# The last block's output projection as seven half-size products per pair of units, with a longer pause between two halves of the scan's outputs

## Chip, cores, metric

The kernel runs on one core of a Trainium2 chip. The metric is the time of one execution on the device in microseconds (us), the median of three runs. The core's engines each take their instructions in order: PE multiplies matrices (PEld loads its weights beside it), DVE, ACT and POOL work on tiles, SP starts DMA transfers. They run beside one another and wait for each other by semaphores.

## What is computed

A decaying scan in chunks over `x` (attention without softmax), whose result goes through a gated two-layer product:

```python
# scan, per batch and head, by chunks: M = (C B^T) * decay, causal
y[:, :, sl] = M @ xc + (C @ state) * decay_to_i
state = decay_full * state + sum(B x decay_from_j)
# y, regrouped to 3072 tokens of 256, is the x of
g = x @ w_gate                       # 256 -> 1536
val = x @ w_val                      # 256 -> 1536
out = (g * sigmoid(g) * val) @ w_out # 1536 -> 256
```

All of it is fp32. A product of two fp32 matrices is made of three products of their rounded high parts and the remainders: w_high·x_high, w_high·x_low, w_low·x_high. So each operand is split first: ACT rounds it to the high part, and DVE or POOL subtracts that from the whole for the low part.

## The kernel before

The tokens go in 6 blocks, k = 0 to 5, of 512 columns. For each, the scan writes four tiles y (`S`, `L`, `st` and `y` in the trace), and the gated product follows. The hidden layer is cut into 12 slices of 128, two slices making a pair j = 0 to 5. From block 3 on, gate and value of a pair are computed by seven products of half size each (units (k, j, m), m = 0 gate, m = 1 value; `stage1a`, `stage1b`, `stage2`, `stage3`): PE writes tile `pq` and tile `r`, ACT copies (`sp<-pq`), POOL adds (`sp<-sp`, the function `both`), DVE subtracts (`sp<-r,sp`, `carry`) and finishes (`pq<-pq,sp`; `hp<-pq,hp`). The result is the pair's hidden tile `hp`, 128 x 4 x 256 columns, in fp32.

`pair_high` (ACT, 128x1024) and two `pair_low` (POOL, 128x512) split it into `ph` and `pl`. Then `project` multiplies by the output weights `wo`, high and low: per slice and per half m of the outputs three matmuls of 512 columns, summed over the 12 slices in the PSUM banks `po5_0` and `po5_1`. In the last block the last four slices (HB = 4) of `po5_1` go in two halves of 256 columns. That makes 60 matmuls of 512 columns and 24 of 256. ACT and DVE copy the banks to `ob` (`drain`, `drain_part`), and SP stores these (`store`).

No loop sets the order on the engines: every step is added to a `Plan` with an engine (or `EITHER(pool, dve)`, two engines with a cost on each), a cost, a due time, what it needs, and the slots it takes and gives back. The plan simulates the engines and writes each one's order, which `Ordered` then keeps; all operations pass through its line, L206 in the trace (L205 after the change). Steps of the pretended engine `Page` are pauses: one stands between the two halves of the outputs y of a block (`values_and_sums`, `carried_and_values`), and in it PE takes other matmuls, those of the block before.

Of the kernel before, what the change touches and what calls it, by code (L numbers as in the profile page):

```python
# [9 lines left out]
F32 = mybir.dt.float32  # L10
# [17 lines left out]
NP = H // 2  # L28
NF = DFF // P
SG = 23  # L30
HB = 4
RAW = 8
PR = 3
FAST = 3
# [182 lines left out]
def scan_moe_kernel(ctx: ExitStack, tc, aj, an, bc, xb, wgv, wo, cst, own, first_e, e_table, out):  # L217
# [654 lines left out]
    def pair_low(k, j, i):  # L872
# [47 lines left out]

    def sums_of(k):

        if k < NB - 1:
            return [(m, (0, T), (f,)) for f in range(NF) for m in range(2)]
        early, late = NF - HB, tuple(range(NF - HB, NF))
        runs = [(0, (0, T)), (1, (0, T // 2)), (1, (T // 2, T))]
        return [(m, (0, T), (f,)) for f in range(early) for m in range(2)] + [(m, t, late) for m, t in runs]

    def project(k, m, t, fs):
        if (k, m) not in tot:  # L930
            tot[k, m] = ps_mm.tile([P, T], F32, tag="mm", name=f"po{k}_{m}")
        for f in fs:
            r, e = divmod(f, 2)
            o = tot[k, m][:, t[0] : t[1]]
            if k < FAST:
                hh, hl = (hid[k, f][n][:, t[0] : t[1]] for n in ("hh", "hl"))
            else:
                a = slice(t[0] // TH, t[1] // TH)
                hh, hl = (
                    hid[k, r, n].rearrange("p (a b) t -> p a b t", b=2)[:, a, 1 - e] for n in "hl"  # L940
                )
# [10 lines left out]
    def drain(k, m, t, e):  # L952
        obs[k, m, t] = moe.tile([P, T], F32, tag="ob", name=f"ob{k}_{m}_{t[0]}", bufs=2)
        copy(e, obs[k, m, t][:, : t[1] - t[0]], tot[k, m][:, t[0] : t[1]])

    def drain_part(k, m, t, i, e):
        if (k, m, t) not in obs:
            obs[k, m, t] = moe.tile([P, T], F32, tag="ob", name=f"ob{k}_{m}_{t[0]}", bufs=2)
        n = (t[1] - t[0]) // 2
        copy(e, obs[k, m, t][:, n * i : n * i + n], tot[k, m][:, t[0] + n * i : t[0] + n * i + n])  # L960

    def store(k, m, t):
        sp.dma_start(out[k, P * m : P * m + P, t[0] : t[1]], obs[k, m, t][:, : t[1] - t[0]])
# [31 lines left out]
    def do(f, *a):  # L995
# [83 lines left out]
    def fast_x(k, z, y, done):  # L1079
# [7 lines left out]
        for n, (i, ms) in enumerate(((2, ()), (1, ("M1",)), (0, ("M3",)), (3, ("M4",)))):  # L1087
# [42 lines left out]
    for k in range(NB):  # L1130
# [132 lines left out]
    for k in range(NB):  # L1263
        prev = None
        for n, (m, t, fs) in enumerate(sums_of(k)):
            b = ("po", k, m)
# [7 lines left out]
            if fs[-1] == NF - 1:  # L1274
                o = ("ob", k, m, t)
                c = 0.6 * (t[1] - t[0]) / T
                if t[0]:
                    parts = [("ob", k, m, t, i) for i in range(2)]
                    add("-", 0.0, lambda: None, r, [prev], takes=[("ob", o)], gives=("held", o))
                    for i, e in enumerate(("Act", "DVE")):  # L1280
                        add([(e, c / 2)], None, do(drain_part, k, m, t, i), r + 0.5, [("held", o)], uses=[b, o], gives=parts[i])
                    add("SP", 0.48, do(store, k, m, t), r + 2, parts, uses=[o], gives=("stored", k, m, t), lag=0.9)
                    continue
                add([("Act", c)] + ([("DVE", c)] if k < FAST - 1 or k == NB - 1 else []), None, do(drain, k, m, t), r + 0.5, [prev], takes=[("ob", o)], uses=[b, o], gives=o)
# [147 lines left out]
```

## Time and profile before

| what | value |
| --- | --- |
| median of three runs | 339.67 us (338.07, 341.18, 339.67) |
| the profiled execution: its time, its span | 338.35 us, 336.6 us |
| mean granted clock of PE in it | 1.000 of full speed |
| PE busy | 329.8 us |
| DVE, ACT, POOL busy | 230.7, 175.8, 177.5 us |

The span runs from the first to the last instruction; the profiled execution's own time is 1.75 us above it. Busy times are of the whole span; a stage may have another limit.

### The profile page before, as it was taken

The page shows a single profiled execution, that of the slowest core. Times are in us where ns is not written, and L with a number is a line of the kernel's source. Part 1 is how long each engine was busy: PE and PEld are TensorE (multiplying, and loading weights), DVE is VectorE, ACT ScalarE, POOL GpSimd, SP SyncE. Part 2 cuts the span into 40 slices and gives each one's busy share as a digit, 9 for nine tenths or more (in the row PEclk, how much of TensorE's full clock was granted, in tenths as well). Part 3 has the DMA queues.
Part 4 walks back from the last instruction along what each step waited for, and adds up shares of the span by engine and source line. Part 5 has one row for each costly group of instructions (what it writes and reads, how often), then busy time and mean ns, then how long its engine had stood idle before and what let it go on. Part 6 is the DMA issues. An engine that isn't in the chain of part 4 may idle for free.

```text
span 336.6 us, 8407 instructions
## 1 busy us (share of the span) xinstructions
PE 329.8 (98%) x3506; PEld 276.0 (82%) x3506; DVE 230.7 (69%) x410; ACT 175.8 (52%) x324; POOL 177.5 (53%) x164
## 2 busy tenths in 40 slices
PE   7999999999999999999999999989999999999995
PEld 5645758888888888878888999868999878999985
DVE  7999999879699981475298577735777834376600
ACT  5797967654245534544382666312666342566411
POOL 2487743510223009897979998350368341368450
PEclk9999999999999999999999999999999999999999
DMA  7899986990001841000292000008400000100001
GB/s 247 288 384 238 293 182 209 248 220 19 1 2 44 194 145 63 1 2 2 52 233 82 14 2 2 2 4 232 148 1 0 5 2 2 62 2 0 2 0 62
DMA packets 10100, 31.05 MB, mean 92 GB/s; under 512 B 1455, under 2 KB 2223, under 8 KB 9423
## 3 DMA queue, kind: packets, MB, share of 16 engines
q1 hardware_dynamic: 7192, 24.21, 24.0%
q0 software_dynamic: 1440, 2.88, 4.8%
q10 hardware_dynamic: 1431, 3.43, 3.5%
q8 instruction: 27, 0.44, 0.5%
q14 instruction: 10, 0.08, 0.1%
HBM read 24.29 MB, written 3.35 MB: 82 GB/s over the span
## 4 chain that ended last, share of the span: by engine, by line
PE 98%; DMA 1%; issue 0%; DVE 0%; ACTq 0%; ACT 0%
PE gv L206 31%; PE po L206 30%; PE pq L206 23%; PE y L206 6%; PE r L206 4%; PE S L206 2%; PE a L206 1%; DMA rows<-in_aj 1%; PE st L206 0%; ACTq L1426 0%; PE rest L206 0%; DVE rows L206 0%; PE e L206 0%; DVE ob L206 0%; ACT ob L206 0%
## 5 line engine op out<-in xcount | busy, mean ns | idle before, releaser
L206 POOL TENSOR_TENSOR pl<-hp,ph 128x512 fp32r<-128x512 f32 x36 | 46.6, 1306 | 28.7 <-PE po L206 24.2
L206 POOL TENSOR_TENSOR sp<-sp 128x256 f32<-128x256 f32 x36 | 27.7, 772 | 33.1 <-ACT sp L206 30.9
L206 DVE TENSOR_TENSOR pq<-pq,sp 128x512 f32<-128x512 f32 x36 | 25.0, 697 | 21.5 <-PE pq L206 21.5
L206 ACT COPY sp<-pq 128x512 f32<-128x512 f32 x36 | 20.9, 588 | 22.9 <-PE pq L206 22.7
L206 DVE TENSOR_TENSOR_SCAN L<-L,dj 128x520 f32<-128x520 f32 x20 | 27.1, 1399 | 4.9 <-DMA L<-clipped 4.9
L206 ACT ACTIVATE sg<-gv 128x512 f32<-128x512 f32 x36 | 21.4, 596 | 15.8 <-PE gv L206 15.4
L206 DVE TENSOR_TENSOR sg<-gv,sg 128x512 f32<-128x512 f32 x28 | 19.1, 683 | 11.1 <-PE gv L206 8.3
L206 ACT ACTIVATE hp<-pq 128x512 f32<-128x512 f32 x36 | 20.1, 601 | 10.5 <-DVE pq L206 8.9
L206 ACT COPY ob<-po 128x512 f32<-128x512 f32 (+2 forms) x13 | 7.0, 545 | 35.1 <-PE po L206 34.6
L206 DVE TENSOR_TENSOR hp<-pq,hp 128x512 f32<-128x512 f32 x36 | 23.5, 681 | 1.0 <-PE pq L206 0.6
L206 DVE TENSOR_TENSOR sp<-r,sp 128x256 f32<-128x256 f32 x36 | 15.0, 416 | 13.2 <-POOL sp L206 13.2
L206 ACT CAST ph<-hp 128x1024 fp32r<-128x1024 f32 x18 | 18.9, 1054 | 9.6 <-PE po L206 6.1
L206 ACT CAST hh<-sg 128x512 fp32r<-128x512 f32 x23 | 14.3, 622 | 14.0 <-PE po L206 9.7
L206 DVE TENSOR_TENSOR hh<-sg,hh 128x512 fp32r<-128x512 f32 x28 | 20.6, 760 | 0.8 <-ACT hh L206 0.7
L206 DVE TENSOR_TENSOR L<-S,L 128x512 f32<-128x512 f32 x24 | 15.1, 682 | 1.0 <-PE S L206 1.0
L206 PE MATMUL y<-L,xb 64*32 64x64 f32 x768 | 11.7, 232 | 1.0 <-issue 0.9
L206 PEld LDWEIGHTS y<-L,xb 64*32 64x32 f32 x768 | 9.2, 109 | 4.1 <-issue 1.7
L206 DVE TENSOR_TENSOR gv<-gv,sg 128x512 f32<-128x512 f32 x8 | 5.6, 700 | 10.1 <-PE gv L206 10.1
L206 ACT ACTIVATE Cz<-bc,cs 128x512 f32<-128x512 f32 x12 | 8.0, 716 | 4.6 <-DMA bc<-in_bc 4.6
L206 POOL TENSOR_TENSOR wt<-wg0h,wg0l 128x512 f32<-128x512 f32 x1 | 1.3, 1290 | 16.7 <-DVE xb L206 16.7
L206 POOL TENSOR_TENSOR wdl<-wd,wdh 128x512 fp32r<-128x512 f32 x6 | 8.2, 1366 | 3.6 <-ACT wdh L206 3.6
L206 DVE COPY ob<-po 128x128 f32<-128x128 f32 x1 | 0.3, 290 | 14.2 <-ACT ob L206 14.2
(673 smaller groups left out, 1118.3 us busy)
## 6 DMA issues: line engine op xcount, KB each, us to landing
L<-clipped SPq DMA_DIRECT2D x10, 520.0 KB, 10.3
xb<-in_xb SPq DMA_DIRECT2D x6, 768.0 KB, 12.3
bc<-in_bc SPq DMA_DIRECT2D x6, 512.0 KB, 5.9
out<-ob SPq DMA_DIRECT2D x11, 256.0 KB, 4.5
E<-clipped SPq DMA_DIRECT2D x5, 260.0 KB
wg0r<-in_wgv SPq DMA_DIRECT2D x1, 512.0 KB
wg1r<-in_wgv SPq DMA_DIRECT2D x1, 512.0 KB, 6.3
wg2r<-in_wgv SPq DMA_DIRECT2D x1, 512.0 KB
```

Of the source, the lines that this page charges most:

```text
L206: ins = getattr(self.engine, name)(*a, **k)
```

## The change

The last block's projection is computed as seven products of half size per pair, M1 to M7, in place of eight. One side of each product is a quarter of `wo` (M1, M2, M4) or a sum of quarters (M5, M7, M6, M3); the other is a quarter of `hp` or a mix of quarters. Three matmuls of 256 columns for each product and pair make 126 matmuls, summed over the pairs in four banks `pm0` to `pm3`.

- Sums of weights, per pair: `o_whole` adds high and low (128x512), four `o_sum` (128x128), `o_high` on ACT and `o_low` (128x512) split them into `os`. `o_whole` and `o_low` stand on POOL for pairs 0 and 4, and 0 and 5, and on DVE for the others; they use `spare` and `spare2`, tiles where the scan's `L` and `xb` were.
- Mixes of the hidden tile, per pair, all on DVE: "ends" (128x512), then "both" (128x256, into `hp`), then "last" (128x256).
- `pair_high` and `pair_low` give way to four `h_high` (ACT) and four `h_low` per pair, three of 128x512 and one of 128x256. The parts lie where weights lay that no step needs any more: `wg0h`, `wg0l` and so on, `ws`, `wdh`, `wdl`. The plan puts the low parts of 18 of the 24 on POOL, six on DVE (`wg1l`, `wdh1`, `wg7l`, `wdl4`, `wdh4`, `wg11l`).
- `join`: one copy on ACT and seven adds of 128x256 on DVE make the four quarters of the output from the banks; four stores of 128x256 follow.
- The pause between the two halves of y, from block 4 on, goes from 0.5 to REST = 2.8, and the slack of `values_and_sums` from 1.0 to 0.1. Ahead of the first half of y of block 4, PE then has four groups of three `po` matmuls (before: six), and six between the halves (before: four). For block 5 it is three groups and six (before: five and four).
- One idle matmul near the start is 256 columns wide (before: 512).

The core of the diff (the steps' costs in the plan, `new_spare` with the views of the tiles, and most of `join` are cut):

```diff
-HB = 4
+    PRODUCTS = ("M1", "M2"), ("M6", "M7"), ("M5", "M3"), ("M4",)
+    FACTORS = dict(M1=(0, 1), M2=(0, 0), M3=(1, 0), M4=(3, 0), M5=(2, 0), M6=(1, 1), M7=(2, 1))
+    SUMS = dict(M6=0, M7=1, M5=2, M3=3)
...
+    def o_whole(r, e):
+        flat = [w[r].rearrange("p a b c -> p (a b c)").bitcast(F32) for w in (woh, wol)]
+        (ge if e == "Pool" else ve).tensor_tensor(out=spare["whole"][r % 2], in0=flat[0], in1=flat[1], op=ALU.add)
...
+        one, two, how = {
+            "M5": (a21, a22, ALU.add), "M7": (a21, a11, ALU.subtract),
+            "M6": (s[:, 2], a11, ALU.subtract), "M3": (a12, s[:, 0], ALU.subtract),
+        }[n]
+        (ge if e == "Pool" else ve).tensor_tensor(out=s[:, SUMS[n]], in0=one, in1=two, op=how)
...
+    def h_mix(j, n):
+        h, t = hid[NB - 1, j, "pair"], spare["mixed"][j % 2]
+        if n == "ends":
+            ve.tensor_tensor(out=t[:, :2], in0=h[:, 3:].to_broadcast([P, 2, TH]), in1=h[:, 1:3], op=ALU.subtract)
+        elif n == "both":
+            ve.tensor_tensor(out=h[:, 3], in0=h[:, 2], in1=t[:, 0], op=ALU.subtract)
+        else:
+            ve.tensor_tensor(out=t[:, 2], in0=h[:, 0], in1=h[:, 3], op=ALU.subtract)
+
+    def h_parts(j, i):
+        flat = [w[f] for f in (2 * j, 2 * j + 1) for w in (wgh, wgl)] + [wsum[j][n] for n in ("s", "dh", "dl")]
+        flat = [t.rearrange("p a b c -> p a (b c)") for t in flat]
+        h, t = hid[NB - 1, j, "pair"], spare["mixed"][j % 2]
+        src = (h[:, :2], h[:, 2:], t[:, :2], t[:, 2:])[i]
+        return (*((flat[i], flat[4 + i]) if i < 3 else (flat[3][:, :1], flat[3][:, 1:])), src)
...
+    def h_low(j, i, e):
+        hi, lo, src = h_parts(j, i)
+        (ge if e == "Pool" else ve).tensor_tensor(out=lo, in0=src, in1=hi.bitcast(F32), op=ALU.subtract)
+
+    def project_mixed(i, j):
+        if not j:
+            bank[i] = ps_mm.tile([P, 2, TH], F32, tag="mm", name=f"pm{i}")
+        for q, n in enumerate(PRODUCTS[i]):
...
+            c, o = FACTORS[n]
+            hi, lo, _ = h_parts(j, c)
+            for p, (w, h) in enumerate(((wh, hi), (wh, lo), (wl, hi))):
+                te.matmul(
+                    bank[i][:, q], w, h[:, o], start=not (j or q or p), stop=j == NF // 2 - 1 and p == 2,
+                    skip_group_check=True,
+                )
...
+    def join(n):
...
+        one, u = mix_in[0][:, 0], mix_in[1]
+        to, b, q, more = {
+            "00": (obs[k, 0][:, :TH], 0, 1, one),
...
+        }[n]
+        ve.tensor_tensor(out=to, in0=bank[b][:, q], in1=more, op=ALU.add)
...
-    def drain_part(k, m, t, i, e):
...
-        times, wide = (1, 512) if n else (4, 64)
+        times, wide = (1, 256) if n else (4, 64)
...
+            if k == NB - 1:
+                split_mixed(j, r, ready, pair)
+                continue
             add("Act", 1.1, do(pair_high, k, j, "Act"), r, ready, takes=[("raw", h)], uses=[pair], gives=("qhh", k, j))
...
-            add("PE", 1.41, do(values_and_sums, k), z + 11, [("page", k, 0), *mixed, ("bt", k)], takes=[("at", i) for i in y], uses=[L, XB, *y], gives=("st", k, BATCH - 1), kind="f", slack=SLACK)
-            add("Page", PAGE if k <= FAST else 0.5, lambda: None, z + 11, [("st", k, BATCH - 1)], gives=("page", k, 1))
+            add("PE", 1.41, do(values_and_sums, k), z + 11, [("page", k, 0), *mixed, ("bt", k)], takes=[("at", i) for i in y], uses=[L, XB, *y], gives=("st", k, BATCH - 1), kind="f", slack=SLACK if k <= FAST else 0.1)
+            add("Page", PAGE if k <= FAST else REST, lambda: None, z + 11, [("st", k, BATCH - 1)], gives=("page", k, 1))
...
+REST = 2.8
```

Two places in the order of the instructions. The first is the units of block 5. DVE there, while pairs 2 and 3 are computed (names as above: `pq5_2_0` is the gate's tile of pair 2), before:

```order
L206 TENSOR_TENSOR hp5_2_3805<-pq5_2_1_3775,hp5_2_3805 128x512
L206 TENSOR_TENSOR pq5_2_0_3743<-pq5_2_0_3743,sp5_2_0_3758 128x512
L206 TENSOR_TENSOR sp5_3_0_3824<-r5_3_0_3827,sp5_3_0_3824 128x256
L206 TENSOR_TENSOR pq5_2_1_3775<-pq5_2_1_3775,sp5_2_1_3790 128x512
L206 TENSOR_TENSOR sp5_3_1_3856<-r5_3_1_3860,sp5_3_1_3856 128x256
L206 TENSOR_TENSOR hp5_2_3805<-pq5_2_1_3775,hp5_2_3805 128x2x256
```

and after, where `spare` is the tile of the mixes and `wdh1` takes a low part of pair 1:

```order
L205 TENSOR_TENSOR spare_3587<-hp5_1_3793 128x512
L205 TENSOR_TENSOR pq5_2_1_3822<-pq5_2_1_3822,sp5_2_1_3837 128x512
L205 TENSOR_TENSOR sp5_3_1_3908<-r5_3_1_3911,sp5_3_1_3908 128x256
L205 TENSOR_TENSOR hp5_2_3853<-pq5_2_1_3822,hp5_2_3853 128x2x256
L205 TENSOR_TENSOR hp5_3_3924<-pq5_3_1_3893,hp5_3_3924 128x512
L205 TENSOR_TENSOR pq5_3_0_3857<-pq5_3_0_3857,sp5_3_0_3876 128x512
L205 TENSOR_TENSOR hp5_1_3793<-hp5_1_3793,spare_3587 128x256
L205 TENSOR_TENSOR spare_3587<-hp5_2_3853 128x512
L205 TENSOR_TENSOR sp5_4_0_3944<-r5_4_0_3947,sp5_4_0_3944 128x256
L205 TENSOR_TENSOR spare_3587<-hp5_1_3793 128x256
L205 TENSOR_TENSOR pq5_3_1_3893<-pq5_3_1_3893,sp5_3_1_3908 128x512
L205 TENSOR_TENSOR wdh1_1758<-hp5_1_3793,wg2l_542 128x512
```

Four mixes and one low part stand between the units' own operations, each with all its inputs in SBUF. POOL at the same place, before:

```order
L206 TENSOR_TENSOR pl5_1_3858<-hp5_1_3741,ph5_1_3839 128x512
L206 TENSOR_TENSOR sp5_3_1_3856<-sp5_3_1_3856 128x256
L206 TENSOR_TENSOR pl5_1_3858<-hp5_1_3741,ph5_1_3839 128x512
L206 TENSOR_TENSOR sp5_4_0_3890<-sp5_4_0_3890 128x256
L206 TENSOR_TENSOR pl5_2_3924<-hp5_2_3805,ph5_2_3905 128x512
```

and after, where `ws`, `wdl` and `wg` are low parts of the mixed tiles:

```order
L205 TENSOR_TENSOR ws1_1824<-hp5_1_3793,wg2h_540 128x512
L205 TENSOR_TENSOR wdl1_1759<-spare_3587,wg3h_582 128x512
L205 TENSOR_TENSOR sp5_4_0_3944<-sp5_4_0_3944 128x256
L205 TENSOR_TENSOR ws2_1989<-hp5_2_3853,wg4h_595 128x512
L205 TENSOR_TENSOR sp5_4_1_3975<-sp5_4_1_3975 128x256
L205 TENSOR_TENSOR wdl2_1900<-spare_3587,wg5h_603 128x512
```

A pair's two low parts `pl` have become three or four low parts between the `sp` additions, and two low parts of 128x512 can stand in a row.

The second place is what follows the units. DVE from the last half of pair 5's hidden tile on, before:

```order
L206 TENSOR_TENSOR hp5_5_4003<-pq5_5_1_3973,hp5_5_4003 128x512
L206 TENSOR_TENSOR pq5_5_0_3940<-pq5_5_0_3940,sp5_5_0_3956 128x512
L206 TENSOR_TENSOR pq5_5_1_3973<-pq5_5_1_3973,sp5_5_1_3988 128x512
L206 TENSOR_TENSOR hp5_5_4003<-pq5_5_1_3973,hp5_5_4003 128x2x256
L206 COPY ob5_1_256_4135<-po5_1_4027 128x128
```

and after:

```order
L205 TENSOR_TENSOR hp5_5_4099<-pq5_5_1_4038,hp5_5_4099 128x2x256
L205 TENSOR_TENSOR spare_3587<-hp5_4_4026 128x512
L205 TENSOR_TENSOR spare_3587<-hp5_5_4099 128x512
L205 TENSOR_TENSOR hp5_4_4026<-hp5_4_4026,spare_3587 128x256
L205 TENSOR_TENSOR wdl4_2204<-spare_3587,wg9h_650 128x512
L205 TENSOR_TENSOR spare_3587<-hp5_4_4026 128x256
L205 TENSOR_TENSOR wdh4_2203<-hp5_4_4026,wg8l_894 128x512
L205 TENSOR_TENSOR hp5_5_4099<-hp5_5_4099,spare_3587 128x256
L205 TENSOR_TENSOR spare_3587<-hp5_5_4099 128x256
L205 TENSOR_TENSOR ob5_0_4204<-pm0_4073,join0_4206 128x256
L205 TENSOR_TENSOR wg11l_859<-spare_3587,wg11l_859 128x256
L205 TENSOR_TENSOR join1_4207<-pm1_4128,join0_4206 128x256
```

Nine operations stand between the hidden tile and the first `join` of bank `pm1`, seven of them ahead of and including "both" of pair 5 (`hp5_5<-hp5_5,spare`). POOL at the end, before:

```order
L206 TENSOR_TENSOR pl5_3_3990<-hp5_3_3871,ph5_3_3971 128x512
L206 TENSOR_TENSOR sp5_5_1_3988<-sp5_5_1_3988 128x256
L206 TENSOR_TENSOR pl5_3_3990<-hp5_3_3871,ph5_3_3971 128x512
L206 TENSOR_TENSOR pl5_4_4066<-hp5_4_3937,ph5_4_4050 128x512 x2
L206 TENSOR_TENSOR pl5_5_4078<-hp5_5_4003,ph5_5_4055 128x512 x2
```

and after:

```order
L205 TENSOR_TENSOR wdl3_2118<-spare_3587,wg7h_613 128x512
L205 TENSOR_TENSOR ws4_2244<-hp5_4_4026,wg8h_616 128x512
L205 TENSOR_TENSOR wdh3_2117<-hp5_3_3924,wg6l_863 128x512
L205 TENSOR_TENSOR ws5_2421<-hp5_5_4099,wg10h_755 128x512
L205 TENSOR_TENSOR wdl5_2342<-spare_3587,wg11h_855 128x512
L205 TENSOR_TENSOR wg9l_653<-spare_3587,wg9l_653 128x256
L205 TENSOR_TENSOR wdh5_2341<-hp5_5_4099,wg10l_760 128x512
```

POOL's last instruction, `wdh5`, is the low part of "both" of pair 5; after it PE still has 30 of the 126 matmuls, and 72 stand between the units' last product and these.

## Rows read from the trace of the kernel before

**Rows 1.** The page: busy time of the engines; chain that ended last, by engine.

```profile
PE 329.8 (98%) x3506; PEld 276.0 (82%) x3506; DVE 230.7 (69%) x410; ACT 175.8 (52%) x324; POOL 177.5 (53%) x164
...
PE 98%; DMA 1%; issue 0%; DVE 0%; ACTq 0%; ACT 0%
```

**Rows 2.** Windows of the last block: units, projection (start:end, length, then each engine).

```profile
284.00:316.00 32.00, 32.00 (x261) 31.44 (x259) 17.24 (x33) 17.98 (x29) 18.89 (x20) 1.00 0.05 17
316.00:333.00 17.00, 16.89 (x89) 14.41 (x87) 2.49 (x4) 3.26 (x5) 5.04 (x4) 1.00 0.04 15
```

**Rows 3.** Timeline, PE, last block: start, duration, engine, line, instruction, [idle before <-releaser].

```profile
304.84 0.28 PE L206 MATMUL pq<-xh5a,wg6h 128*128 128x256 f32 x1
...
315.38 0.28 PE L206 MATMUL pq<-xl5b,wdh 128*128 128x256 f32 x1
...
317.59 0.40 PE L206 MATMUL po<-ph,wo0h 128*128 128x512 f32 x1
...
318.98 0.39 PE L206 MATMUL po<-ph,wo1h 128*128 128x512 f32 x1
...
329.86 0.28 PE L206 MATMUL po<-ph,wo4h 128*128 128x256 f32 x1
...
332.61 0.28 PE L206 MATMUL po<-ph,wo5l 128*128 128x256 f32 x1
```

**Rows 4.** Timeline, ACT and DVE, after the last matmul.

```profile
332.92 0.54 ACT L206 COPY ob<-po 128x256 f32<-128x256 f32 x2 [2.28 <-PE po L206]
...
333.50 0.29 DVE L206 COPY ob<-po 128x128 f32<-128x128 f32 x1 [14.21 <-ACT ob L206]
```

**Rows 5.** Timeline, PE, outputs y of block 4 and y of block 5.

```profile
219.11 0.80 PE L206 MATMUL y<-L,xb 64*32 64x64 f32 x60
...
226.01 0.32 PE L206 MATMUL y<-L,xb 64*32 64x64 f32 x10 [0.88 <-issue]
...
275.92 0.86 PE L206 MATMUL y<-L,xb 64*32 64x64 f32 x64
```

**Rows 6.** Timeline, POOL and then DVE, block 4, about 250 to 261.

```profile
251.31 1.30 POOL L206 TENSOR_TENSOR pl<-hp,ph 128x512 fp32r<-128x512 f32 x1 [0.61 <-ACT ph L206]
252.56 1.20 POOL L206 TENSOR_TENSOR sp<-sp 128x256 f32<-128x256 f32 x1
...
251.95 1.22 DVE L206 TENSOR_TENSOR bc<-bc,E 128x512 f32<-128x512 f32 x1
...
260.60 0.68 DVE L206 TENSOR_TENSOR xb<-xb,L 128x512 f32<-128x512 f32 x1
```

**Rows 7.** Timeline, DVE, one pair of units of block 5 and the next.

```profile
309.30 0.70 DVE L206 TENSOR_TENSOR pq<-pq,sp 128x512 f32<-128x512 f32 x1 [1.46 <-PE pq L206]
309.91 0.41 DVE L206 TENSOR_TENSOR sp<-r,sp 128x256 f32<-128x256 f32 x1
310.24 1.28 DVE L206 TENSOR_TENSOR hp<-pq,hp 128x512 f32<-128x512 f32 x2
311.79 0.70 DVE L206 TENSOR_TENSOR pq<-pq,sp 128x512 f32<-128x512 f32 x1 [0.27 <-PE pq L206]
...
314.27 0.70 DVE L206 TENSOR_TENSOR pq<-pq,sp 128x512 f32<-128x512 f32 x1 [1.46 <-PE pq L206]
...
318.59 0.69 DVE L206 TENSOR_TENSOR hp<-pq,hp 128x512 f32<-128x512 f32 x1
```

**Rows 8.** Timeline, POOL, block 5.

```profile
288.02 0.74 POOL L206 TENSOR_TENSOR sp<-sp 128x256 f32<-128x256 f32 x1 [9.22 <-ACT sp L206]
...
310.74 0.74 POOL L206 TENSOR_TENSOR sp<-sp 128x256 f32<-128x256 f32 x1 [0.37 <-ACT sp L206]
312.08 1.30 POOL L206 TENSOR_TENSOR pl<-hp,ph 128x512 fp32r<-128x512 f32 x1 [0.61 <-ACT ph L206]
```

**Rows 9.** The page, group of ACT: rounding a 128x512 tile.

```profile
L206 ACT CAST hh<-sg 128x512 fp32r<-128x512 f32 x23 | 14.3, 622 | 14.0 <-PE po L206 9.7
```

**Rows 10.** Timeline, DVE, mixes ahead of y of block 4.

```profile
214.85 2.48 DVE L206 TENSOR_TENSOR L<-S,L 128x512 f32<-128x512 f32 x4 [0.30 <-PE S L206]
```

More of the change, by code (lines that the diff above doesn't have):

```diff
@@ new lines, in o_high, with o_low @@
+    def o_high(r):
+        t = osum[r]["t"] = raw.tile([P, 2, 4 * P], F32R, tag="wraw", name=f"os{r}")
+        se.copy(t[:, 0], spare["sums"][r % 2])
+    def o_low(r, e):
+        t = osum[r]["t"]
+        (ge if e == "Pool" else ve).tensor_tensor(
+            out=t[:, 1], in0=spare["sums"][r % 2], in1=t[:, 0].bitcast(F32), op=ALU.subtract
+        )
[7 more added lines that the diff above has]
+            ve.tensor_tensor(out=t[:, 2], in0=h[:, 0], in1=h[:, 3], op=ALU.subtract)
@@ new lines, in join @@
+    def join(n):
+        k = NB - 1
+        if n == "first":
+            for m in range(2):
+                obs[k, m] = moe.tile([P, T], F32, tag="ob", name=f"ob{k}_{m}", bufs=2)
+            for q in range(2):
+                mix_in[q] = moe.tile([P, 2, TH], F32, tag="sg", name=f"join{q}", bufs=SG)
+            se.copy(mix_in[0][:, 0], bank[0][:, 0])
+            return
+        one, u = mix_in[0][:, 0], mix_in[1]
+        to, b, q, more = {
+            "00": (obs[k, 0][:, :TH], 0, 1, one),
+            "16": (u[:, 0], 1, 0, one),
+            "167": (u[:, 1], 1, 1, u[:, 0]),
+            "11": (obs[k, 1][:, TH:], 2, 0, u[:, 1]),
+            "165": (mix_in[0][:, 1], 2, 0, u[:, 0]),
+            "01": (obs[k, 0][:, TH:], 2, 1, mix_in[0][:, 1]),
+            "10": (obs[k, 1][:, :TH], 3, 0, u[:, 1]),
+        }[n]
+        ve.tensor_tensor(out=to, in0=bank[b][:, q], in1=more, op=ALU.add)
@@ L921, in sums_of @@
     def sums_of(k):
[L923 to L927, printed above, removed]
+        return [(m, (0, T), (f,)) for f in range(NF) for m in range(2)]
     def project(k, m, t, fs):
@@ L999, in scan_moe_kernel @@
     plan = Plan(
-        dict(mm=4, at=4, L=1, E=1, bc=1, xb=1, Cz=1, T=2, raw=RAW, w=1, xh=2, xl=2, sg=SG, ob=2, pair=PR),
+        dict(mm=4, at=4, L=1, E=1, bc=1, xb=1, Cz=1, T=2, raw=RAW, w=1, xh=2, xl=2, sg=SG, ob=2, pair=PR, mixed=2, whole=2, sums=2),
         dict(SP=3.3, Act=3.0, DVE=1.0, PE=1.5, Pool=2.0, Page=0.0, **{"-": 0.7}),
@@ L1091, in fast_x, with split_mixed @@
             add("DVE", d, do(x_split_low, k, i), z + 17.5 + 0.9 * n, [("xsh", k, i)], uses=[y[i]], gives=("xsl", k, i))
+    def split_mixed(j, r, ready, pair):
+        tt = ("mixed", j)
+        for n, c, need, take in (
+            ("ends", 0.69, [*ready, "spare"], [("mixed", tt)]), ("both", 0.42, [("hm", j, "ends")], []), ("last", 0.42, [("hm", j, "both")], [])
+        ):
+            add("DVE", c, do(h_mix, j, n), r, need, takes=take, uses=[pair, tt], gives=("hm", j, n))
+        for i, of in ((0, None), (2, "ends"), (1, "both"), (3, "last")):
+            c = (0.6, 1.29, 0.69) if i < 3 else (0.36, 0.75, 0.42)
+            mine = [tt if i > 1 else pair]
+            add("Act", c[0], do(h_high, j, i, "Act"), r + 0.2 * i, [("hm", j, of)] if of else ready, uses=[*mine, *sums_held(j)], gives=("hmh", j, i))
+            add(EITHER(*c[1:]), None, do(h_low, j, i), r + 1 + 0.2 * i, [("hmh", j, i)], uses=[*mine, *sums_held(j)], gives=("hml", j, i))
@@ new lines, in last_sums, with after @@
+    def last_sums():
+        k = NB - 1
+        add("-", 0.0, new_spare, due(k) - 1, [("y", k)], takes=[("L", "spare"), ("xb", "spare")], gives="spare")
+        for j in range(NF // 2):
+            r = due(k, 2 * j) + 4
+            w, s = ("ow", j), ("osum", j)
+            add(EITHER(1.4, 0.69), None, do(o_whole, j), r, ["spare", ("ql", k - 1, NF // 2 - 1), ("wh", NF + j), ("wl", NF + j)], takes=[("whole", w)], gives=("ow", j))
+            for n, need, take in (("M5", "ow", [("sums", s)]), ("M7", "M5", []), ("M6", "M7", []), ("M3", "M6", [])):
+                add(EITHER(0.5, 0.28), None, do(o_sum, j, n), r + 0.2, [("ow", j) if need == "ow" else ("os", j, need)], takes=take, uses=[w, s], gives=("os", j, n))
+            add("Act", 0.6, do(o_high, j), r + 0.3, [("os", j, "M3")], takes=[("raw", ("os", j))], uses=[s], gives=("osh", j))
+            add(EITHER(1.29, 0.69), None, do(o_low, j), r + 0.4, [("osh", j)], uses=[s], gives=("osl", j))
+        for i, ns in enumerate(PRODUCTS):
+            prev = None
+            for j in range(NF // 2):
+                r = due_sum(k, 3 * i) + 0.1 * j
+                need = [("hml", j, FACTORS[n][0]) for n in ns] + [("osl", j) for n in ns if n in SUMS]
+                add("PE", 0.355 * len(ns), do(project_mixed, i, j), r, need + ([prev] if prev else []), takes=[] if j else [("mm", ("bank", i))], uses=[("bank", i), *sums_held(j)], gives=("pm", i, j), kind="r")
+                prev = ("pm", i, j)
+        def after(i):
+            return ("pm", i, NF // 2 - 1)
+        r = due_sum(k, NF)
+        add("Act", 0.36, do(join, "first"), r, [after(0)], takes=[("ob", ("ob", k, 0)), ("ob", ("ob", k, 1)), ("sg", "join"), ("sg", "join2")], uses=[("bank", 0)], gives=("join", "first"))
+        for n, b, need in (
+            ("00", 0, ["first"]), ("16", 1, ["first"]), ("167", 1, ["16"]), ("11", 2, ["167"]), ("165", 2, ["16"]), ("01", 2, ["165"]), ("10", 3, ["167"]),
+        ):
+            add("DVE", 0.42, do(join, n), r + b, [after(b), *(("join", x) for x in need)], uses=[("bank", b)], gives=("join", n))
+            if len(n) == 2 and n != "16":
+                add("SP", 0.48, do(store_mixed, int(n[0]), int(n[1])), r + 2, [("join", n)], gives=("stored", k, n), lag=0.9)
@@ L1276, in scan_moe_kernel @@
                 c = 0.6 * (t[1] - t[0]) / T
[L1277 to L1284, printed above, removed]
+                add([("Act", c)] + ([("DVE", c)] if k < FAST - 1 else []), None, do(drain, k, m, t), r + 0.5, [prev], takes=[("ob", o)], uses=[b, o], gives=o)
                 add("SP", 0.48, do(store, k, m, t), r + 2, [o], uses=[o], gives=("stored", k, m, t), lag=0.9)
```

31 lines of the change are left out of this document (25 added, 6 removed).

## The prediction

> **What bounds the kernel now.** I read the busy times and the chain that ended last first [rows 1]: PE is busy for 98% of the span and is 98% of the chain. So an edit gains only what it takes out of PE's queue, and loses only where PE comes to wait. The windows of the last block come next [rows 2]. While the units run (284 to 316), PE is busy for all of 32.00 us, and DVE, ACT and POOL for 17 to 19 each. In the projection DVE works for 2.49 of 17 us. By busy time there is room for everything that the change adds; the timelines of DVE and POOL have to say whether it is room that can be used.
>
> **PE's columns.** In the units, 90 matmuls of 256 columns start between 304.84 and 315.38, 0.1184 us apart. In the projection, 48 of 512 columns start between 318.98 and 329.86, 0.2267 apart, and 24 of 256 from 329.86 to 332.61, 0.1196 apart [rows 3]. The old projection is 60 x 0.2267 + 24 x 0.1196 = 16.47 us. The new one is 126 x 0.1184 to 0.1196 = 14.92 to 15.07. That takes 1.4 to 1.55 off; I take 1.5. (The half-size idle matmul near the start saves at most 0.11, the difference of the two distances; counted as nothing.)
>
> **The end.** After the last matmul (332.61 + 0.28) ACT copies 128x256, then 128x128, and DVE the other 128x128, which ends at 333.79: 0.90 us [rows 3, 4]. The new end is one DVE add of 128x256 out of PSUM, as `sp<-r,sp` with 0.41 [rows 7], and the 0.03 from matmul to copy: 0.44. That is 0.45 off. The four stores go from SP, where only the last is on the path, as before.
>
> **The longer pause.** The second half of y of block 4 has 0.88 us in which PE waits for nothing that the profile shows; the same matmuls of block 5 run through (64 in one piece) [rows 5]. With six groups of `po` between the halves instead of four, 1.4 us more lies between them, and the code ahead of it shifts. Between a gain of nothing and 0.88 I take 0.88, since block 5's row has none. The Trainium skill ("Runtime: NRT & Kernel Launch", section "Instruction fetch mechanics") says that the sequencer streams its code in blocks, and that crossing a boundary is mostly hidden; the row's idle time doesn't look hidden, if it is that at all, but by the page the pause would be worth nothing, and the sum 0.9 higher. The price of the pause: y's first half comes 1.4 us earlier. It waits for the mixes `L<-S,L`, which end at 214.85 + 2.48 = 217.33, and PE came to it at 219.11 [rows 5, 10]; 217.7 still is behind them, by 0.4. Nothing, then.
>
> **What DVE and POOL do to each other.** This is the term that decides. In block 4 DVE's `bc<-bc,E` (128x512, both inputs in SBUF) began at 251.95 while POOL's `pl` ran until 252.61; it ended at 253.17 and took 1.22 us, where the like `xb<-xb,L` took 0.68. POOL's `sp<-sp`, begun at 252.56, took 1.20 and ended at 253.76, where an undisturbed one takes 0.74 [rows 6, 8]. So the two didn't run together: each waited for the other's end. Behind the other's end DVE needed 0.56 and POOL 0.59 (253.76 − 253.17); a 128x512 of POOL then holds the other up for some 1.15 (two halves of 0.59, less what overlaps) and a 128x256 of DVE for 0.28. Meanwhile `pq<-pq,sp`, `hp<-pq,hp` and `sp<-r,sp`, which take one input from PSUM, keep to 0.70, 0.64 and 0.41 beside POOL's additions [rows 7, 8]. The last block of the kernel before has only such operations on DVE. The change puts 18 mixes and six low parts there, all with both inputs in SBUF, and gives POOL more to do.
>
> The Trainium skill ("SBUF — State Buffer", section "Who interferes with whom") has the same as a lock held for the whole instruction. The rows say less: 0.56 of 0.68 was left to do when POOL let go. By the page's whole durations the waits below would be some 15% longer, and the sum 0.9 us higher.
>
> Units: one pair takes 4.97 us (309.30 to 314.27), in which DVE idles for 1.46 + 0.27 = 1.73 [rows 7]. Four pairs are mixed while the next ones are computed: 6.9 us of room; 24 matmuls of the first bank (2.84 us) stand ahead of pair 5's last products where 6 x 0.2267 = 1.36 stood, which makes it 8.4. DVE's own new work there is 4 x (0.69 + 0.41 + 0.41) = 6.0 for the mixes and 0.41 + 0.69 + 0.41 for three low parts: 7.5. Room of 0.9 is left, with no waiting. These are 15 operations. POOL has eleven of 128x512 and nine of 128x256 beside them: 11 x 1.15 + 9 x 0.6 = 18.1 us of holding in 21.3 (4 x 4.97 + 1.5) and what is added, say 70% of the time. An operation that meets one finds on average (11 x 1.15² + 9 x 0.6²) / (2 x 18.1) = 0.49 left. So DVE waits for 15 x 0.7 x 0.49 = 5.1 and ends the units 4.3 us late. From below: the two engines together hold 18.1 + 5.5 = 23.6 us in 21.3, so 2.3 late even without a gap. From above, when each meets one: 15 x 0.49 − 0.9 = 6.5.
>
> Projection: the units' last half of `hp` ends some 1.7 us after its last matmul (318.59 + 0.69 against 317.59, where `po` followed) [rows 3, 7], and 72 matmuls, 8.5 us, cover what comes before `wdh5` is needed: 6.8 left. In it must go seven operations of DVE up to "both" of pair 5 (4 x 0.56 + 3 x 0.28 = 3.1), three of POOL (2 x 1.15 + 0.6 = 2.9) that exclude them, ACT's rounding (0.62 [rows 9]) and `wdh5` (1.30 [rows 8]): 7.9, so 1.1 late. Alone, without POOL's three, it would be 5.0 and hidden. What DVE is late at the end of the units comes on top, since nothing after them lets it catch up. Queued behind are ACT's `h_high`, POOL's low parts and, on PE, everything behind the product that waits.
>
> Weight sums: they stand ahead of the units, where POOL idles for 9.22 us [rows 8]. No row shows a POOL addition of 128x128; between a quarter and all of the 0.74 of 128x256, 16 of them are 3 to 12 us, and two `o_whole` and two `o_low` 5.2. Most of it fits; between nothing and 1 us I take 0.5, nearer to the lower since PE has `po` and `gv` ahead.
>
> **The sum.** On the profiled execution: 338.35 − 1.5 − 0.45 − 0.88 + 4.3 + 1.1 + 0.5 = 341.4, that is +3.1. On the median of 339.67, which is 1.3 above that execution, **342.7 us**. Waits on PE from 2.3 to 8.6 (6.5 + 1.1 + 1.0) and a pause worth 0.88 or nothing give 339.1 to 346.3 on that scale.
>
> **The rivals.** *Hidden.* DVE and POOL delay each other, but PE's banks and the order let it go on; then only the gains stay: 339.67 − 2.83 = 336.8, or 337.7 if the pause gives nothing. For it: DVE is idle for nearly half of the units, and 4.97 us per pair have room for all the own work. Against: the holdings alone exceed the room. Chance 0.17.
>
> *A closed loop, slower.* POOL's queue keeps `sp<-sp` of the next unit behind a low part, which waits for ACT's rounding, which waits for DVE's mix, which waits for POOL's operation in progress; and DVE's `sp<-r,sp` waits for that `sp<-sp`. Then nothing overlaps: per pair 2 x 0.6 + 3 x 1.15 of POOL, 1.1 + 0.3 of DVE, and POOL's two waits of 0.37 and 0.61 for ACT [rows 8] make 7.0 instead of 4.97, 8.2 over four pairs, less the 1.5 of pair 5; with 1.1 and 0.5 against 2.83 the sum is +5.5: 345.2. It decides from the point where a mix is late by more than POOL's slack of about 1 us per pair. Chance 0.17.
>
> *It doesn't do what it says.* The idle 0.88 comes back in another place (block 5's y, or the shifted code), or y now outruns the mixes, whose margin is 0.4: some 0.9 to 1.5 above the forecast, 344. Chance 0.1. The forecast itself (waits between 3.5 and 7.5) has 0.56.
>
> **How the numbers follow.** About 1%, 3.4 us, is what a measurement here can tell: faster is below 336.3, slower above 343.1. Faster holds the better half of the hidden case, where the gains are also larger than taken: 0.09. Slower holds the closed loop, most of the third rival and two fifths of the forecast case: 0.17 + 0.08 + 0.2 = 0.45. The rest, 0.46, is within 1%. The range goes from 338.0, which leaves out most of the hidden case, to 346.3, the upper end of the waits, which leaves out what the closed loop makes of a second cause on top: 0.2 outside.
>
> **What would show it.** Right: matmuls of `pm` 0.118 to 0.120 apart; one DVE add of about 0.42 behind the last; no 0.88 in y of block 4; DVE's mixes of 128x512 at 1.0 to 1.8 instead of 0.69, POOL's `sp` often at 1.2; PE idle in the units by 2 to 4 us (released by ACT or DVE) and ahead of `pm1` by 1 to 3 (released by DVE or POOL). Wrong: PE without idle time ahead of `pq` and `pm`, which would mean that the waits are covered; or mixes at their 0.69, which would mean that such mixes and POOL run side by side after all, and the kernel lands near 336.8.

## The result, and the profile after

The changed kernel takes 344.24 us (median of 16 runs, 342.02 to 346.44) where the kernel before takes 339.86 (16 runs): ratio 1.013, interval 1.0104 to 1.0156, so 4.4 us slower. Forecast were 342.7 and a loss of 3.1. Ratios, here and below, are of the fast executions alone, so they can differ from the quotient of two medians, which take every execution. The profiled execution took 343.18 us with a span of 341.4, 4.8 above the span of before; it is split up below.

The page of the changed kernel, busy time and the chain that ended last (to compare with [rows 1]):

```profile
PE 330.0 (97%) x3548; PEld 276.9 (81%) x3548; DVE 263.4 (77%) x457; ACT 183.5 (54%) x344; POOL 203.6 (60%) x190
...
PE 76%; DVE 11%; POOL 4%; DMA 4%; issue 2%; ACT 1%; SPq 1%; POOLq 0%; DVEq 0%; ACTq 0%
```

PE's busy time hardly moved (329.8 to 330.0), though it has 1.5 us of columns less to do; DVE has 33 us more, POOL 26. The chain that ended last, which was PE for 98%, is now PE for 76% and DVE for 11%: the end waits for DVE. The windows of the last block (as in [rows 2]):

```profile
284.00:316.00 32.00, 30.49 (x231) 28.71 (x229) 31.35 (x49) 19.87 (x38) 30.35 (x33) 1.00 0.05 17
316.00:339.00 23.00, 20.53 (x166) 19.87 (x165) 20.22 (x34) 10.38 (x20) 15.44 (x13) 1.00 0.06 19
```

DVE and POOL are full in the units, with 31.35 and 30.35 of 32 us. Busy time counts what an operation waits inside itself, which the rows of both engines show; POOL first, then DVE, in the units of block 5:

```profile
311.24 1.49 POOL L205 TENSOR_TENSOR ws<-hp,wg4h 128x512 fp32r<-128x512 f32 x1
312.68 1.18 POOL L205 TENSOR_TENSOR sp<-sp 128x256 f32<-128x256 f32 x1
314.00 1.28 POOL L205 TENSOR_TENSOR wdl<-spare,wg5h 128x512 fp32r<-128x512 f32 x1
...
311.49 1.78 DVE L205 TENSOR_TENSOR spare<-hp 128x512 f32<-128x512 f32 x1
...
313.53 0.62 DVE L205 TENSOR_TENSOR spare<-hp 128x256 f32<-128x256 f32 x1
...
314.68 1.15 DVE L205 TENSOR_TENSOR wdh<-hp,wg2l 128x512 fp32r<-128x512 f32 x1
```

The mix of 128x512 that began at 311.49 ended at 313.27, with 1.78 us instead of 0.69; POOL's `ws` ran until 312.73, and 0.54 after that the mix was done (0.56 in [rows 6]). `sp<-sp`, begun at 312.68, ended 0.59 behind the mix, at 313.86, as in [rows 6]. In these operations the engines take turns. PE's waits, from its timeline:

```profile
239.72 0.39 PE L205 MATMUL pq<-xh4a,wg0h 128*128 128x256 f32 x1 [2.75 <-ACT sp L205]
...
287.84 0.28 PE L205 MATMUL pq<-xh5a,wg0h 128*128 128x256 f32 x1
...
290.52 0.39 PE L205 MATMUL pq<-xh5a,wg0h 128*128 128x256 f32 x1 [0.39 <-ACT sp L205]
...
296.89 0.39 PE L205 MATMUL pq<-xh5a,wg4h 128*128 128x256 f32 x1 [0.25 <-ACT hp L205]
...
315.13 0.39 PE L205 MATMUL pq<-xh5a,wg10h 128*128 128x256 f32 x1 [0.78 <-ACT sp L205]
...
316.57 0.39 PE L205 MATMUL pq<-xh5a,wdh 128*128 128x256 f32 x1 [0.47 <-ACT hp L205]
...
332.14 0.39 PE L205 MATMUL pm<-wdh,os 128*128 128x256 f32 x1 [1.24 <-DVE wdh L205]
```

The first is ahead of block 4's units and has nothing to do with the products (below). The row at 287.84 is block 5's first product. The others I count by starts, 0.118 to 0.12 us being the distance without a wait, up to the second matmul behind the wait, since that one is late too: 0.65 at 290.52, 0.51 at 296.89, 0.33 at 304.71, 1.03 at 315.13, 0.74 at 316.57, 1.50 at 332.14, and about 0.2 each at 295.66, 309.86 and 334.51: 5.3 in block 5. The expectations below have 5.0, a count that left some of the small ones out. The weight sums have 1.3 of it (up to 297), the units 2.3, the projection 1.7.

The end, with PE's last matmul and DVE's last add ([rows 4] before):

```profile
337.96 0.28 PE L205 MATMUL pm<-wg11l,wo5l 128*128 128x256 f32 x1
...
338.28 0.42 DVE L205 TENSOR_TENSOR ob<-pm,join 128x256 f32<-128x256 f32 x1 [0.99 <-PE pm L205]
```

From the end of the last matmul (338.24) to the end of the add there are 0.46 us, forecast 0.44. The pause shows in the second half of y of block 4 and in ACT's next `Cz`, which it makes out of block 5's load of `bc`:

```profile
224.20 0.86 PE L205 MATMUL y<-L,xb 64*32 64x64 f32 x64
...
237.38 1.33 ACT L205 ACTIVATE Cz<-bc,cs 128x512 f32<-128x512 f32 x2 [3.30 <-DMA bc<-in_bc]
```

The 64 matmuls run through; the idle 0.88 of [rows 5] is gone (by starts, the half is 1.1 shorter). But ACT stood 3.30 us ahead of Cz, waiting for block 5's load of `bc`. In the kernel before, the same row of ACT read:

```profile
235.94 1.34 ACT L206 ACTIVATE Cz<-bc,cs 128x512 f32<-128x512 f32 x2 [0.59 <-DMA bc<-in_bc]
```

ACT takes its instructions in order, so its `sp` copies of block 4's first units waited with it, and PE for these: the 2.75 at 239.72. The forecast did not have that.

The sum of this execution, by PE's starts: −1.4 columns, −1.1 y of block 4, −0.2 that PE came to that y earlier, +2.7 behind Cz, +5.3 waits in block 5, −0.55 from PE's last start to the end of the span: +4.8, which is the measured difference of the spans.

### The profile page after: what moved, and what is told of

Its sections match the earlier page's. It is cut to its first block, busy times and chain, and to the rows that moved or that the text cites. A ratio compares the mean times of both kernels' runs of the same rounds, so it can differ in the third digit from the quotient of the medians.

```text
span 341.4 us, 8589 instructions
## 1 busy us (share of the span) xinstructions
PE 330.0 (97%) x3548; PEld 276.9 (81%) x3548; DVE 263.4 (77%) x457; ACT 183.5 (54%) x344; POOL 203.6 (60%) x190
## 4 chain that ended last, share of the span: by engine, by line
PE 76%; DVE 11%; POOL 4%; DMA 4%; issue 2%; ACT 1%; SPq 1%; POOLq 0%; DVEq 0%; ACTq 0%
PE gv L205 31%; PE po L205 19%; PE pq L205 15%; PE y L205 5%; DVE spare L205 4%; DMA bc<-in_bc 3%; PE r L205 2%; DVE hp L205 2%; POOL spare L205 2%; PE pm L205 2%; PE S L205 2%; DVE L L205 1%; DVE pq L205 1%; POOL pl L205 1%; POOL sp L205 1%
## 5 line engine op out<-in xcount | busy, mean ns | idle before, releaser
L205 POOL TENSOR_TENSOR pl<-hp,ph 128x512 fp32r<-128x512 f32 x24 | 31.2, 1313 | 19.7 <-PE po L205 17.7
L205 POOL TENSOR_TENSOR sp<-sp 128x256 f32<-128x256 f32 x36 | 30.0, 839 | 20.0 <-ACT sp L205 19.6
L205 ACT CAST ph<-hp 128x1024 fp32r<-128x1024 f32 x12 | 12.6, 1052 | 7.1 <-PE po L205 4.9
L205 ACT COPY ob<-po 128x512 f32<-128x512 f32 x10 | 5.9, 585 | 18.6 <-PE po L205 18.1
L205 DVE TENSOR_TENSOR spare<-hp 128x512 f32<-128x512 f32 (+1 forms) x12 | 12.5, 1047 | 0.0
```

The source lines that it names most:

```text
L205: ins = getattr(self.engine, name)(*a, **k)
```

## The experiments

The theory: DVE's operations with two inputs in SBUF and POOL's operations exclude each other, and that makes the waits in block 5. Rivals: DVE's queue is too long by its own work; something else of the new projection costs. A second question is the late load. All ratios are to the kernel before, run on the same chip beside it.

**The pause alone**, on the kernel before (the constant REST = 2.8 and the slack of 0.1 go with it and are cut here):

```diff
-            add("Page", PAGE if k <= FAST else 0.5, lambda: None, z + 11, [("st", k, BATCH - 1)], gives=("page", k, 1))
+            add("Page", PAGE if k <= FAST else REST, lambda: None, z + 11, [("st", k, BATCH - 1)], gives=("page", k, 1))
```

> The kernel before with the longer pause alone (REST 2.8, slack 0.1); the old projection stays. Theory one, the late load belongs to the moved order: the idle 0.88 in y of block 4 is gone, and ACT waits some 3 us for the load of bc again, which holds up its copies and then PE by 2.7 before the first unit of block 4; about 1.7 us slower than before, ratio 1.005. Theory two, the late load was a chance of that one execution: only the 0.88 goes, ratio 0.997. Theory three, the pause has its gain and neither: the idle time comes back in another place, ratio 1.000.

0.9979 (0.9940 to 1.0017), 338.99 us. The profiled execution has the gain (64 matmuls of y in one piece) and the late load too (ACT waits 2.70 ahead of Cz), as theory one has it, but the timed runs exclude theory one's 1.005. Either the late load is not in every execution, or the kernel before has it in some of its own; these runs don't tell which.

**The products alone**, the same lines the other way round in the changed kernel:

> The changed kernel with the pause and the slack as before (0.5, 1.0); the seven products stay. Theory one, the late load belongs to the pause: the idle 0.88 stands in y of block 4, no wait of PE ahead of the first unit of block 4, waits of PE in block 5 of about 5 us against gains of 1.95: 3 us slower than before, ratio 1.009, and below the changed kernel by about 1.7 us. Theory two, chance: the same 3 us over before but no less than 0.9 above the changed kernel's own without its chance, so a ratio of 1.009 to 1.012 with the late load seen in one profile or the other.

1.0107 (1.0054 to 1.0160), 343.15 us. ACT waits 0.75 ahead of Cz, the idle time in y is there (0.51), and PE's waits in block 5 are those of the changed kernel and one more, 0.66 by starts at 329.39, ahead of a `pm` matmul that waits for POOL's `ws`. So the loss is the products'; the pause has little part in it.

**One input from PSUM.** The run that tells the theory from its rivals (one of its four lines; the others follow):

```diff
-            ve.tensor_tensor(out=t[:, :2], in0=h[:, 3:].to_broadcast([P, 2, TH]), in1=h[:, 1:3], op=ALU.subtract)
+            ve.tensor_tensor(out=t[:, :2], in0=psum(2), in1=h[:, 1:3], op=ALU.subtract)
```

`psum(n)` is the bank `r` that DVE read last, n times; "both", "last" and DVE's six low parts take one input from it likewise. The mixed tiles then hold other values, so this tells of times alone.

> The changed kernel, but each of DVE's 18 mixes and six low parts takes one input from PSUM (the bank r of a unit that is there) in place of one of the two in SBUF: the mixed tiles hold other values, the output is not the reference's; order, sizes and number of instructions stay, POOL's work too. Theory one, DVE and POOL exclude each other while DVE reads two inputs from SBUF: mixes of 128x512 go from a mean of 1.05 to 0.69, those of 128x256 to 0.41, POOL's sums of 128x256 in the units to 0.74, and of PE's 5.0 us of waits in block 5 those behind 300 us (3.7) go nearly all: 3 to 4 us below the changed kernel. Rival, DVE's queue is too long by its own work and the order of POOL and ACT: the mixes get shorter but PE still waits 3 us or more, at most 1 us below the changed kernel.

0.9992 (0.9954 to 1.0030), 340.19 us: 4.1 below the changed kernel by the medians. The profiled execution, with a late load like the changed kernel's (ACT waits 3.27), is 4.0 shorter (339.21 against 343.18). Groups of DVE and POOL from 284 to 339 us (busy, mean ns of one), in the changed kernel:

```profile
L205 DVE TENSOR_TENSOR spare<-hp 128x512 f32<-128x512 f32 x6 | 7.5, 1270 | 0.0
...
L205 DVE TENSOR_TENSOR spare<-hp 128x256 f32<-128x256 f32 x6 | 4.9, 824 | 0.0
...
L205 DVE TENSOR_TENSOR hp<-hp,spare 128x256 f32<-128x256 f32 x6 | 3.9, 644 | 0.0
...
L205 POOL TENSOR_TENSOR sp<-sp 128x256 f32<-128x256 f32 x12 | 11.6, 968 | 0.2 <-ACT sp L205 0.2
```

and in this run:

```profile
L205 DVE TENSOR_TENSOR spare<-r,hp 128x512 f32<-128x512 f32 x6 | 4.0, 682 | 0.0
...
L205 DVE TENSOR_TENSOR spare<-hp,r 128x256 f32<-128x256 f32 x6 | 2.5, 413 | 0.0
L205 DVE TENSOR_TENSOR hp<-hp,r 128x256 f32<-128x256 f32 x6 | 2.5, 412 | 0.0
...
L205 POOL TENSOR_TENSOR sp<-sp 128x256 f32<-128x256 f32 x12 | 9.8, 823 | 0.5 <-ACT sp L205 0.3 <-PE pq L205 0.2
```

The same operations at the same places take 682 instead of 1270 ns, and 412 instead of 644 to 824; POOL's sums lose 145 ns each on average. PE's waits from 284 us on (total, times, longest), in the changed kernel and then here:

```profile
PE pm L205 <- DVE wdh L205: 1.2, 1, 1.2
PE pq L205 <- ACT sp L205: 1.2, 2, 0.8
PE pq L205 <- ACT hp L205: 0.7, 2, 0.5
...
PE pq L205 <- ACT sp L205: 0.4, 1, 0.4
PE pq L205 <- ACT hp L205: 0.3, 1, 0.3
```

By starts, those behind 297 us are gone, 4.0 of 5.3; what is left is 1.3 from 290 to 297. The rival, which allowed 1 us at most, falls: DVE has as many operations of the same shapes here, in the same order.

**Cz behind**, on the changed kernel:

```diff
-CZ_BEHIND = {3: [("hh", 1, NF - 1)], 5: [("xsl", 4, 0), ("xsl", 4, 3)]}
+CZ_BEHIND = {3: [("hh", 1, NF - 1)], 5: [("cp", 4, 1, 0)]}
```

> The changed kernel with block 5's two Cz of ACT, which wait for the load of bc, put behind the first three sp copies of block 4's units (and one scan of DVE behind its sp); nothing else moves but the order of three groups of PE there. Theory one, what PE lost ahead of block 4's units was ACT standing in its queue for a late load, in most executions: 2 to 2.7 us below the changed kernel. Theory two, the late load was a chance of one execution: no difference beyond 0.5 us. In both, the waits in block 5 stay at 5 us.

1.0096 (1.0058 to 1.0133), 341.93 us. The wait ahead of block 4's units went from 2.75 to nothing over 0.4 in its profile, those in block 5 stayed. By medians it is 2.3 us below the changed kernel, by the ratios 1.2 (1.0096 against 1.0130), and the two ratios' intervals overlap, so the timed gain isn't certain.

**Pause and Cz behind, without the products**, both edits on the kernel before:

> The kernel before with the longer pause, and block 5's two Cz behind the first sp copies of block 4: no seven products. If the idle time in y of block 4 and ACT's wait for the load are the two sides of the pause, both are gone now: 0.9 to 1.2 us below the kernel before, ratio 0.997, and PE without a gap over 0.5 us from 180 us on. If the pause's gain is given back elsewhere whatever ACT does: ratio 1.000.

0.9952 (0.9917 to 0.9986), 338.04 us: faster than both kernels. PE has no wait from 180 us on that the profile lists.

**Cz behind alone**, on the kernel before, the control:

> The kernel before with block 5's two Cz behind the first sp copies of block 4, without the longer pause: the control to the fifth run. If the fifth run's gain is the idle time in y of block 4, which the pause removes, this one keeps that idle time (0.5 to 0.9) and gains at most the 0.2 to 0.4 that PE waits ahead of block 4's units: ratio 0.999 to 1.000. If Cz alone made the fifth run faster: ratio 0.995 to 0.997, and the pause is worth nothing.

0.9966 (0.9942 to 0.9991), 337.65 us. The idle time in y is there:

```profile
225.47 0.32 PE L206 MATMUL y<-L,xb 64*32 64x64 f32 x10 [0.82 <-issue]
```

So I had the shares the wrong way round: most of the fifth run's gain comes with Cz, and what the pause adds (0.9966 to 0.9952) is within the intervals.

**The gains alone.** The third run, with Cz behind and without sums of weights (plain quarters of the weights in their place):

> The changed kernel with all that should cost nothing: DVE's mixes and low parts with one input from PSUM (as in the third run), no sums of weights (the products take plain quarters of the weights in their place; outputs are not the reference's), Cz behind. If the waits have the three causes exclusion, sums and Cz, PE waits less than 0.4 us in block 5, and what is left are the gains: 1.5 of columns, 0.45 at the end, 0.9 in y: 2.9 us below the kernel before, ratio 0.9915. If something else of the change costs time (the 126 matmuls themselves, the join, ACT's extra parts), it shows here: ratio above 0.995.

0.9918 (0.9869 to 0.9967), 335.48 us. PE's timeline has no listed wait from 180 us on. Block 5's first product, the last matmul and the last add:

```profile
284.56 0.28 PE L205 MATMUL pq<-xh5a,wg0h 128*128 128x256 f32 x1
...
329.36 0.28 PE L205 MATMUL pm<-wg11l,wo5l 128*128 128x256 f32 x1
...
329.68 0.42 DVE L205 TENSOR_TENSOR ob<-pm,join 128x256 f32<-128x256 f32 x1 [0.94 <-PE pm L205]
```

The last two are as far apart as forecast. Block 5 takes 44.80 us from its first product to the last matmul, where the changed kernel takes 50.12 (287.84 to 337.96): the 5.3 of waits once more, counted without adding them up. In the kernel before it starts at

```profile
286.38 0.28 PE L206 MATMUL pq<-xh5a,wg0h 128*128 128x256 f32 x1
```

and ends at 332.61 [rows 3], 46.23: the columns are worth 1.43, if nothing waits. The timed ratio alone can't show this, since this run has Cz behind as well, which is worth 0.3% by itself (the run before).

**Projection from PSUM.** As the third run, but for pairs 4 and 5 alone (`if j > 3`):

> The changed kernel with one input from PSUM for the mixes and low parts of pairs 4 and 5 alone (outputs are not the reference's): pairs 0 to 3 stay with two inputs in SBUF. If units and projection lose apart from each other, the wait ahead of bank pm1 (1.5 us) is gone and the waits in the units (0.25 + 0.93 + 0.63) stay: 1.5 us below the changed kernel, ratio to before 1.0085. If DVE's lateness at the end of the units is what the projection waits for, as the prediction has it, half of the 1.5 or more stays: ratio 1.010 to 1.013.

1.0106 (1.0052 to 1.0161), 342.49 us; the six runs don't tell the two expectations apart, the waits of PE from 284 us on do:

```profile
PE pq L205 <- ACT sp L205: 1.2, 2, 0.8
PE pq L205 <- ACT hp L205: 0.7, 2, 0.5
```

There is none for `pm`, while those in the units stand as in the changed kernel. With the units just as late, the projection waits for nothing.

**Units from PSUM**, the complement (`if j < 4`):

> The complement of the seventh run: one input from PSUM for the mixes and low parts of pairs 0 to 3 (outputs are not the reference's); pairs 4 and 5 keep two inputs in SBUF. If units and projection lose apart from each other, the waits in the units (0.25 + 1.03 + 0.74) are gone and the wait ahead of bank pm1 stays at 1.2 us or more: 2 us below the changed kernel, ratio to before 1.006. If the wait in the projection is DVE's lateness carried over from the units, as the prediction has it, both go: ratio 1.001 or less, wait ahead of pm1 below 0.5.

1.0031 (0.9997 to 1.0064), 339.68 us. The same view:

```profile
PE pm L205 <- DVE wdh L205: 0.4, 1, 0.4
PE pq L205 <- ACT sp L205: 0.4, 1, 0.4
PE pq L205 <- ACT hp L205: 0.3, 1, 0.3
```

The waits in the units are gone, and that for `pm` fell from 1.2 (1.7 by starts with its followers) to 0.4 (0.9). Neither expectation is met: about half of it was carried over from the units, half is the projection's own. Counted from block 5's first product to the last matmul, this run takes 3.1 off the changed kernel, the run before 1.7, and both edits together (the run with one input from PSUM) 4.0: the two parts overlap by 0.8.

**The mix in PSUM**, an attempt to keep the whole computation:

```diff
+            e = ends[j] = ps_at.tile([P, 2, TH], F32, tag="at", name=f"mx{j}")
+            for i, to in enumerate((t[:, 0], e[:, 1])):
+                ve.tensor_tensor(out=to, in0=grp[k, j, m]["pq"][:, i], in1=t[:, i], op=ALU.mult)
...
-            ve.tensor_tensor(out=t[:, :2], in0=h[:, 3:].to_broadcast([P, 2, TH]), in1=h[:, 1:3], op=ALU.subtract)
+            for i in range(2):
+                ve.tensor_tensor(out=ends[j][:, i], in0=ends[j][:, 1], in1=h[:, 1 + i], op=ALU.subtract)
...
-            add(EITHER(*c[1:]), None, do(h_low, j, i), r + 1 + 0.2 * i, [("hmh", j, i)], uses=[*mine, *sums_held(j)], gives=("hml", j, i))
+            add(EITHER(*c[1:]) if i != 2 else [("DVE", 0.69)], None, do(h_low, j, i), r + 1 + 0.2 * i, [("hmh", j, i)], uses=[*mine, *sums_held(j)], gives=("hml", j, i))
```

> A way to keep the whole computation with fewer collisions: on the kernel of the fourth run (Cz behind), the last quarter of the hidden tile and the mix ends lie in a PSUM bank per pair; the last half of hp and ends become two DVE operations of 128x256 each, the low part of ends goes to DVE with one input in PSUM. Only last and some low parts of 128x256 still have two inputs in SBUF. DVE's own work per pair rises from 4.8 to some 5.2 of 4.97 us, POOL's falls by 1.3. If exclusion is what costs: PE's waits in block 5 fall from 5 to 2 us or less (1.3 of it the sums of weights), 2.5 to 3 us below the fourth run, ratio to before 0.999 to 1.002. If DVE's own length costs: no better than the fourth run, ratio 1.008 or more.

0.9995 (0.9958 to 1.0031), 338.07 us. PE's waits from 284 us on:

```profile
PE pq L205 <- ACT sp L205: 0.4, 1, 0.4
PE pq L205 <- ACT hp L205: 0.3, 1, 0.3
PE pm L205 <- ACT hp L205: 0.2, 1, 0.2
```

By starts they are 1.3 from 289 to 296 and 0.5 at `pm`. DVE has twelve operations more here than in the changed kernel (two halves in place of one) and three low parts more, and PE none of the long waits: it was not the amount of DVE's work. The seven products, Cz and pause together just break even. Block 5 is 1.8 us longer in this profile than in that of the gains alone, and 1.3 of it are the waits that the weight sums leave.

## Why the prediction was right, and where its sizes were off

**PE's columns and the end**: right by the rows, 1.43 for 1.5 and 0.46 for 0.44 from the last matmul to the end of the last add. That the run of the gains alone is 2.8 us faster (0.9918), where the gains were forecast as 2.83, is in part luck: its interval goes from 1.1 to 4.5 us, and it has the gain of Cz in it, which was no part of the forecast.

**The longer pause**: the idle time went in all profiles with the pause. What it is worth isn't measurable: 0.9979, and 0.9952 against 0.9966 for the pause on top of Cz, all within their intervals. Three profiles without it show the idle time, 0.88, 0.51 and 0.82 us, each time behind the 54th of the 64 matmuls. In all three, PE goes on 2.4 to 2.7 us after a 16 KB transfer of the queue that the page calls "instruction" began (223.30, 224.47 and 222.84 us); in the changed kernel that transfer begins at 221.85, 1.5 us ahead of the half's first matmul. That fits a PE that waits for code, but no run moves the transfer by itself. The Trainium skill ("Runtime: NRT & Kernel Launch", section "Instruction fetch mechanics") has such crossings mostly hidden; these rows are not hidden, if that is what they are, but the timed runs don't tell their worth from nothing.

**What DVE and POOL do to each other**: the mechanism was right and decided the sign. The rows of the changed kernel have 0.54 and 0.59 behind the other's end where [rows 6] have 0.56 and 0.59, and one input from PSUM took 4.0 of 5.3 us away. The Trainium skill ("SBUF — State Buffer", section "Who interferes with whom") states that a DVE instruction with two SBUF inputs contends with a GpSimd (POOL) instruction that reads SBUF, and that one with at most one SBUF input, outside DVE's two-port modes, does not; the 1270 and 682 ns of the same mix agree.

**Its size**: 5.9 forecast, 5.3 in the profile, but spread otherwise. *Units*: 4.3 forecast, 2.3 measured. What DVE loses in its operations was right: the 15 new ones took 12.86 us there and 7.54 in the third run, 5.3 more, forecast 5.1. The term that was mis-sized is the room. From the first mix to the last half of `hp`, DVE was idle for 2.8 us in the third run, where I had counted 0.9, and for 0.6 in the changed kernel: 2.2 of the loss fell into time that was idle anyway. Counted from block 5's first product, DVE ended the units 2.6 us later than in the third run, and PE 2.3 later: most of the lateness that was left did reach PE. *Projection*: 1.1 forecast, 1.7 measured, and 0.9 without the lateness of the units. I had written that the units' lateness comes on top, since nothing lets DVE catch up; the two runs with pairs apart show that it doesn't add up: PE had waited in the units as well, and so was nearly as late. *Weight sums*: 0.5 forecast, 1.3 measured. POOL's 128x128 took 0.46 where nothing held it up and 0.64 on average, and DVE's sums of two SBUF inputs collided with them, which the term had not counted.

**What the forecast did not have**: ACT's queue behind the load of `bc`, 2.7 us in the profiled execution. With Cz in its old place, ACT waited 0.59 and 0.75 without the pause, and 3.30, 2.70, 3.27, 0.78 and 0.57 with it. The long waits are those where the load itself was slow: 10.3, 9.3 and 10.0 us from issue to landing, against 8.3 to 8.6 in the four others. Whether the pause makes it more frequent stays open; that Cz alone made the kernel before faster argues that it falls into some of its executions as well, but no profile of it shows one. The rival "closed loop" (345.2) came out near the median for another reason: POOL's queue stood for ACT's rounding, but PE's waits in block 5 stayed at 5.3, not 8.3. That 342.7 came as near as 1.5 us is in part luck as well: waits 0.6 too large stand against a term that the sum did not have.

## What to carry to other kernels

Before giving an engine more work, look not only at its idle share but at which operations it will meet: two engines that are half idle each can be one resource in the operations that are added. In this kernel an operand in PSUM instead of SBUF was enough to part them. And an instruction that waits for a load belongs behind the work that others wait for in the same queue: moving one pair of instructions gave 0.3%, where the new projection, computed in full, at best broke even.

## What was not expected of the hardware

The same loads landed at different times: from issue to landing, the load of `bc` took 8.4 us in the profile of before and 10.3 in the changed kernel's. And the executions part in the first 40 us: the first `S` of block 1, with 382 matmuls ahead of it in every one, started at 35.1 to 36.6 us in eleven of the twelve profiles and at 39.4 in the fourth run's; the first `S` of block 4 followed 177.9 to 178.8 us later in all twelve. A single profiled time of this kernel is therefore no measure of 1%.
